# An attention and two MLP layers on one core: the MLP's step counter moved one tick forward, and the first loads issued in another order

## The chip, the cores and the metric

The kernel runs on one core of one Trainium2 chip. The metric is device time in microseconds of one execution, from launch to end. The core has five queues that run by themselves and meet at semaphores: PE (TensorE, matrix products), DVE (VectorE), ACT (ScalarE), POOL (GpSimd) and SP (SyncE, which here only issues DMAs). ACT issues a few DMAs too. Each queue works strictly in the order of the program: an instruction that waits holds up all that stands behind it.

## What is computed

Three parts follow each other: attention inside chunks of 64 tokens, a layer with squared ReLU, and a mixture of four experts with given weights.

```python
attn = softmax(q_c @ k_c.T / sqrt(64))          # per head, per chunk of 64 tokens
x = (attn @ v_c)  ->  [2304 tokens, 512]
h = max(x @ w_in, 0); y = (h * h) @ w_out       # w_in, w_out arrive as float64
p = domain_probs / sum
out = sum_e p[:, e] * (max(y @ w1[e], 0) @ w2[e])
```

Every float32 product is made of three products of float32r parts (high x high, high x low, low x high), so each operand is split into a high part and a low rest before use. The float64 weights are first turned into float32 on the chip.

## The kernel before

**Ticks.** Attention and the first MLP layer are woven together in a loop over ticks `r` (lines 895 to 950). The 2304 tokens are 18 tiles of 128. Attention of tile t runs in four stages over three ticks: `s0_stage` (transposes q and k on PE, ACT copies them out; for tile r+1 in tick r), `s1_stage` (scores on PE; DVE takes the maximum and subtracts it, L241 and L242, two of each), `exp_stage` (ACT), `norm_stage` (DVE, L253 to L256, in the next tick), `s2_stage` (transposes of the probabilities, PE and ACT, two ticks later), `s3_stage` (product with v on PE; ACT writes the high part of x at L283, DVE the low part at L284).

**Steps.** The first layer is cut into 80 steps `m`, four passes over five blocks of tokens (384, 384, 512, 512, 512) and four columns of w_in each. Step m runs in tick r = m + `LEAD`. In it `l1(m)` makes 12 matmuls into a PSUM bank (L300), ACT applies ReLU (L311), DVE squares (L312), ACT and DVE split the result (L316, L317); `l2(m-1)` makes 12 matmuls of the step before (L333). Until tick 20 `l1` always takes the one bank of tag "h" (`psh`), which the next `l1` can enter only when L311 and L312 have read it. `LEAD` is 5: tokens 0 to 383 are tiles 0 to 2, tile 2 goes through `s3_stage` in tick 4, so step 0 in tick 5 is the first that finds its block of x.

**Weights.** A unit is a 128-wide piece of w_in or w_out (512 KB as float64). `unit_load` brings it in, `unit_convert` makes it float32 (two ACT operations, L131 and L132; four on DVE, L133, L136, L141, L144; two on POOL, L145 and L146), `unit_split` splits it one tick later (ACT L153, POOL L154). `FIRST` gives the tick of conversion of the eight units of the first pass, in the order of `order`: one in each of ticks 0 to 7. The load of a unit stands two ticks ahead of its conversion. `SECOND` does the same around the end of attention (ticks 17 to 24), `UOFF` for the later passes, relative to `LEAD`. `JOBS` are ticks in which preparation of the second layer's weights starts.

**Order within a tick.** DMAs of the tick on SP; scores of tile r; normalisation of tile r-1; first half of the conversions; three quarters of `l1`; `s2`; `s0` of q; the last quarter of `l1` with ReLU and square, and a quarter of `l2`; `s0` of k; second half of the conversions; a quarter of `l2`; `s3`; exp; splits of units; the split of the step's result and the rest of `l2`. The banks for scores and transposes are taken from eight in turn while m < 0 (`tags = "ttthaaaa"`) and from three after that (`"t"`).

**Start.** The identity matrix is built on POOL, PE runs eight warming matmuls on it, and the first loads are issued from SP and ACT in turns:

```python
two = (nc.sync, nc.scalar)
run_all([load_qk(0, two)])        # q of tile 0 on SP, k on ACT
unit_load(*order[0])              # SP
run_all([load_qk(1, two)])
unit_load(*order[1])              # SP
run_all([load_v_chunk(0, c, two) for c in range(2)])
```

The later loads are all on SP. The program gives each DMA one of eight completion semaphores in turn, so an issue waits until the DMA eight places earlier has landed.

Of the kernel before, what the change touches and what calls it, by code (L numbers as in the profile page):

```python
# [10 lines left out]
F32 = mybir.dt.float32  # L11
# [7 lines left out]
P = 128  # L19
# [2 lines left out]
G = 4  # L22
LAG = 1
RING = 6
LEAD = 5
QK_BUFS = 3
ACC_EARLY = 3
FIRST = [0, 1, 2, 3, 4, 5, 6, 7]
WARM = 8
SECOND = [-3, -2, -1, 1, 0, 2, 3, 4]  # L30
RAW_BUFS = 4
# [2 lines left out]
NSUP = 3  # L34
LAG_A = 2
UOFF = [1, 3, 5, 16, 8, 17, 18, 19]
JOBS = [23, 26, 29, 32, 35, 44, 47, 50, 53, 56, 64, 67, 70, 73, 76, 79]
PLAIN = 16
SWAP = 67

# [6 lines left out]
def tile_kernel(ctx, tc, q, k, v, moe_w_in, moe_w_out, moe2_p, moe2_w1, moe2_w2, out):  # L47
    nc = tc.nc
# [156 lines left out]
    def load_v_chunk(b, c, engines):  # L205
        if b not in vt:
            new_v(b)
        for x in range(2):
            engines[x].dma_start(
                out=vt[b][x * CH:(x + 1) * CH, :, c, :],  # L210
                in_=v[b, x::2, c * CH:(c + 1) * CH, :].rearrange("j k d -> k j d"),
            )
            yield
# [599 lines left out]
    def run_all(loads):  # L813
        for y in loads:
            if hasattr(y, "__next__"):
                for _ in y:
                    pass

    with tc.manual_schedule():
        ident = const.tile([P, P], F32, name="ident")  # L820
        make_identity(nc, ident)
        warm = bank("t")
        for _ in range(WARM):
            nc.tensor.matmul(warm[:, :P], lhsT=ident, rhs=ident, start=True, stop=True)

        two = (nc.sync, nc.scalar)
        run_all([load_qk(0, two)])
        unit_load(*order[0])
        run_all([load_qk(1, two)])
        unit_load(*order[1])  # L830
        run_all([load_v_chunk(0, c, two) for c in range(2)])
        def load_dp():
            late["dp"] = late["x"].tile([P, NTILE, E], F32, name="dp")
            nc.sync.dma_start(out=late["dp"], in_=moe2_p.rearrange("(t p) e -> p t e", p=P))
# [9 lines left out]
                out=prob, in0=dp, in1=psum_.to_broadcast([P, NTILE, E]), op=ALU.mult  # L844
            )

        at(NTILE + 14, "load", load_dp)
        at(NTILE + 20, "split", probs)

        def mlp(m):  # L850
            if 0 <= m < NS:
# [43 lines left out]
        for r in range(LEAD + NS + LAG):  # L895
            m = r - LEAD
            tags = "ttthaaaa" if m < 0 else "t"
            ch = mlp(m) if m >= 0 else iter(())
            if r == NTILE + LAG_A:
                att.close()  # L900
                late["x"] = ctx.enter_context(tc.tile_pool(name="xq", bufs=1, side="right"))
# [5 lines left out]
            if r < NTILE + LAG_A:  # L907
                if r < NTILE:
                    s1_stage(r, tags)
                if 0 <= r - 1 < NTILE:  # L910
                    norm_stage(r - 1)
                conv = do(r, "convert")
                for c in conv:
                    next(c)
                run(ch, 3)
                if 0 <= r - LAG_A:
                    s2_stage(r - LAG_A, tags)
                if r + 1 < NTILE:
                    s0_stage(r + 1, tags, 0)
                run(ch, 2)  # L920
                if r + 1 < NTILE:
                    s0_stage(r + 1, tags, 1)
                for c in conv:
                    run(c)
                run(ch, 1)
                if 0 <= r - LAG_A:
                    s3_stage(r - LAG_A, tags)
                if r < NTILE:
                    exp_stage(r)
                do(r, "split")  # L930
            else:
                if r == SWAP:
                    staging.close()
                    late["raw"] = raw_pool.enter_context(tc.tile_pool(name="raw", bufs=1, reuse_waits="tile"))
                for fn, args in early.pop(r, ()):
                    fn(*args)
                if r > y0_at:
                    next(late.setdefault("y0", y_combine(0)), None)
                if m < NS:
                    run(ch, KD + 2)  # L940
                    conv = do(r, "convert")
                    for c in conv:
                        next(c)
                    run(ch, 1)
                    for c in conv:
                        run(c)
                    do(r, "split")
# [101 lines left out]
```

## Time and profile before

| | us |
|---|---|
| median of three runs | 1227.51 (1227.33 to 1228.13) |
| the profiled execution | 1227.66 |
| its span, first to last instruction | 1225.9 |
| PE busy | 1201.9 (98%) |
| DVE busy | 799.3 (65%) |
| ACT busy | 586.3 (48%) |
| POOL busy | 688.2 (56%) |

The profiled execution lies 0.15 above the median; 1.76 us of it lie outside the span. The page's shares are means over stages that differ: the first 50 us, where attention has no MLP to run beside it, look unlike the rest, so they have to be read by stretches.

### The profile page before, as it was taken

What the parts mean: (1) busy time and instruction counts of PE and PEld (TensorE: products, weight loads), DVE (VectorE), ACT (ScalarE), POOL (GpSimd) and SP (SyncE); (2) the same over time, 40 slices, a digit from 0 to 9 for tenths busy, and PEclk for the clock granted to TensorE, in tenths of its full rate; (3) what the DMA queues carried; (4) which work ended last, traced back from release to release, by engine and by line L of the source; (5) the groups of instructions that cost most, each with busy time, mean ns of one, the idle gap of its engine ahead of it and who ended that gap; (6) DMA issues with size and microseconds to landing.
All of it is one profiled execution on the core that took longest, in us unless ns stands there. A gap on an engine that the chain in (4) does not pass through costs nothing.

```text
span 1225.9 us, 20909 instructions
## 1 busy us (share of the span) xinstructions
PE 1201.9 (98%) x7912; PEld 1108.7 (90%) x7912; DVE 799.3 (65%) x1336; ACT 586.3 (48%) x1172; POOL 688.2 (56%) x650
## 2 busy tenths in 40 slices
PE   7899999999999999999999999999999999999997
PEld 5798888889888988898889889999999999999996
DVE  6966666656747566355555555676767776767676
ACT  5654555534534335533333345454445654545453
POOL 3510157717735465766776644666756766566665
PEclk7999999999999999999999999999999999999999
DMA  9955033552462645555555448666666676666653
GB/s 207 197 124 146 18 91 115 182 189 86 172 216 88 203 155 190 196 189 189 189 189 189 171 152 324 256 255 251 247 248 257 245 291 243 241 241 246 250 226 112
DMA packets 134709, 238.38 MB, mean 194 GB/s; under 512 B 64720, under 2 KB 109776, under 8 KB 128464
## 3 DMA queue, kind: packets, MB, share of 16 engines
q1 hardware_dynamic: 131984, 236.39, 55.8%
q8 instruction: 62, 1.02, 0.3%
q10 hardware_dynamic: 2624, 0.66, 0.3%
q14 instruction: 39, 0.32, 0.1%
HBM read 173.58 MB, written 63.44 MB: 193 GB/s over the span
## 4 chain that ended last, share of the span: by engine, by line
PE 89%; DVE 6%; DMA 2%; issue 1%; ACT 1%; POOL 1%; DVEq 0%; ACTq 0%; SPq 0%; POOLq 0%
PE pst L563 23%; PE psa L658 18%; PE psa L333 15%; PE psa L675 11%; PE pst L300 9%; PE psh L300 6%; PE psh L563 4%; DMA k<-in_k 2%; PE pst L276 1%; PE pst L220 1%; PE pst L235 1%; DVE uw L713 1%; PE pst L262 0%; DVE o L757 0%; DVE o L756 0%
## 5 line engine op out<-in xcount | busy, mean ns | idle before, releaser
L563 PE MATMUL pst<-ar 128*128 128x384 f32 x1728 | 344.5, 336 | 0.4 <-ACT u L596 0.4
L563 PEld LDWEIGHTS pst<-ar 128*128 128x128 f32 x1728 | 295.7, 188 | 8.0 <-ACT u L596 0.7
L333 PE MATMUL psa<-ar 128*128 128x512 f32 (+1 forms) x960 | 219.3, 372 | 1.6 <-ACT ar L316 0.8
L333 PEld LDWEIGHTS psa<-ar 128*128 128x128 f32 x960 | 173.6, 188 | 27.7 <-ACT ar L316 2.2
L589 POOL TENSOR_TENSOR ar<-s,ar 128x384 fp32r<-128x384 f32 x128 | 129.7, 1024 | 64.5 <-ACT ar L588 62.6
L675 PE MATMUL psa<-ar 128*128 128x512 f32 x576 | 149.0, 394 | 0.0
L658 PE MATMUL psa<-ar 128*128 128x256 f32 x1008 | 140.4, 283 | 1.7 <-DVE uw L707 0.7
L658 PE MATMUL psa<-w2x,ar 128*128 128x256 f32 x1008 | 135.6, 279 | 3.2 <-DVE uw L711 2.4
L658 PEld LDWEIGHTS psa<-ar 128*128 128x128 f32 x1008 | 134.4, 188 | 3.7 <-DVE uw L713 1.6
L658 PEld LDWEIGHTS psa<-w2x,ar 128*128 128x128 f32 x1008 | 130.8, 189 | 4.8 <-DVE uw L711 2.6
L145 POOL TENSOR_TENSOR raw<-raw 128x512 f32<-128x512 f32 x32 | 34.3, 1073 | 179.1 <-DVE raw L144 73.3
L689 DVE SCALAR_TENSOR_TENSOR o<-psa,prob,o 128x512 f32<-128x512 f32 x90 | 67.6, 751 | 94.2 <-PE psa L675 94.1
L300 PE MATMUL pst<-ar 128*128 128x512 f32 (+1 forms) x576 | 127.2, 369 | 0.0
L675 PEld LDWEIGHTS psa<-ar 128*128 128x128 f32 x576 | 106.6, 188 | 16.8 <-DVE ar L578 0.2
L596 ACT COPY u<-pst 128x384 f32<-128x384 f32 x144 | 69.4, 482 | 103.5 <-PE pst L563 101.9
L300 PEld LDWEIGHTS pst<-ar 128*128 128x128 f32 x576 | 105.4, 188 | 14.3
L607 ACT ACTIVATE ar<-psh 128x384 fp32r<-128x384 f32 x96 | 47.2, 492 | 140.9 <-DVE psh L603 74.1
L725 POOL TENSOR_TENSOR o<-o,x 128x256 f32<-128x256 f32 x89 | 70.4, 791 | 70.5 <-ACT x L721 68.3
L511 POOL TENSOR_TENSOR ar<-raw,ar 128x896 fp32r<-128x896 f32 x32 | 68.0, 2126 | 74.4 <-ACT ar L510 74.4
L588 ACT CAST ar<-s 128x384 fp32r<-128x384 f32 x128 | 65.5, 513 | 61.6 <-DVE s L584 59.0
L300 PE MATMUL psh<-ar 128*128 128x512 f32 (+1 forms) x384 | 88.9, 373 | 0.4 <-DVE ar L284 0.4
L713 DVE TENSOR_TENSOR uw<-psa,uw 128x512 f32<-128x512 f32 x96 | 63.4, 688 | 31.4 <-PE psa L658 20.6
(132 smaller groups left out, 1899.9 us busy)
## 6 DMA issues: line engine op xcount, KB each, us to landing
ar<-w1d SPq DMA_DIRECT2D x32, 1792.0 KB, 7.3
w2d<-jsplit SPq DMA_DIRECT2D x64, 448.0 KB, 3.5
w1d<-ar SPq DMA_DIRECT2D x16, 1792.0 KB, 8.4
ar<-w2d SPq DMA_DIRECT2D x32, 896.0 KB, 7.9
w2x<-w2d SPq DMA_DIRECT2D x32, 896.0 KB, 8.1
raw<-in_moe_w_in SPq DMA_DIRECT2D x16, 512.0 KB, 4.7
raw<-in_moe_w_out SPq DMA_DIRECT2D x16, 512.0 KB, 5.0
raw<-in_moe_w SPq DMA_DIRECT2D x16, 512.0 KB, 4.4
```

The source lines that it names most:

```text
L300: nc.tensor.matmul(ph[:, :T], lhsT=w[:, kk, :], rhs=x[tb][:, kk, :], start=(kk == 0 and n == 0), stop=(kk == KD - 1 and n == 2),)
L333: nc.tensor.matmul(o, lhsT=w, rhs=y, start=(f == 0 and n == 0), stop=(f == G - 1 and n == 2))
L511: nc.gpsimd.tensor_tensor(out=l, in0=a, in1=h.bitcast(F32), op=ALU.subtract)
L563: nc.tensor.matmul(p, lhsT=w[:, kk, :], rhs=y[:, kk, :], start=(kk == 0 and z == 0 and u in (0, 1, 3)), stop=(kk == 1 and z == 2 and u in ...
L588: nc.scalar.copy(h, st[n, nm])
L589: nc.gpsimd.tensor_tensor(out=l, in0=st[n, nm], in1=h.bitcast(F32), op=ALU.subtract)
L596: nc.scalar.copy(s, d if at == 3 else b)
L658: nc.tensor.matmul(p, lhsT=w, rhs=y, start=(k in (1, 7) and z == 0), stop=(k in (3, 4) and z == 2), skip_group_check=True,)
L675: nc.tensor.matmul(p, lhsT=w[:, ts], rhs=y[:, i, :], start=(i == 0 and z == 0), stop=(i == 1 and z == 2))
L689: nc.vector.scalar_tensor_tensor(out=o, in0=p, scalar=pe, in1=o, op0=ALU.mult, op1=ALU.add)
L713: nc.vector.tensor_tensor(out=uw, in0=pb[n, t, 0], in1=uw, op=ALU.add)
L725: nc.gpsimd.tensor_tensor(out=o1[:, :2 * P], in0=o1[:, :2 * P], in1=x, op=ALU.add)
```

## The change

`LEAD` becomes 4, and step 0 is not run in its tick 4 but whole at the head of tick 5's MLP work, ahead of step 1, which is in tick 5 now. So from step 1 on every step runs one tick sooner against attention. The conversions of units (1,1), (3,0), (2,1) and (3,1) move one tick sooner, so that tick 3 has two and tick 7 none; their loads move with them. `JOBS`, and the two small pieces of the second layer, move by one with the steps; `SECOND` and `SWAP` stay at their ticks. At the start, a tile of one column is set by POOL ahead of the identity and copied onto itself by ACT, which makes ACT load its function table there; q and k of tiles 0 and 1 are all issued on SP, and the first two chunks of v (four DMAs) all on ACT, behind that copy.

```diff
-LEAD = 5
+LEAD = 4
-FIRST = [0, 1, 2, 3, 4, 5, 6, 7]
+FIRST = [0, 1, 2, 3, 3, 4, 5, 6]
-JOBS = [23, 26, 29, 32, 35, 44, 47, 50, 53, 56, 64, 67, 70, 73, 76, 79]
+JOBS = [22, 25, 28, 31, 34, 43, 46, 49, 52, 55, 63, 66, 69, 72, 75, 78]
...
     with tc.manual_schedule():
+        dot = const.tile([P, 1], F32, name="dot")
+        nc.gpsimd.memset(dot, 1.0)
         ident = const.tile([P, P], F32, name="ident")
         make_identity(nc, ident)
...
-        two = (nc.sync, nc.scalar)
-        run_all([load_qk(0, two)])
+        one = (nc.sync, nc.sync)
+        run_all([load_qk(0, one)])
+        nc.scalar.copy(dot, dot)
+        run_all([load_v_chunk(0, c, (nc.scalar, nc.scalar)) for c in range(2)])
         unit_load(*order[0])
-        run_all([load_qk(1, two)])
+        run_all([load_qk(1, one)])
         unit_load(*order[1])
-        run_all([load_v_chunk(0, c, two) for c in range(2)])
...
-        at(NTILE + 14, "load", load_dp)
-        at(NTILE + 20, "split", probs)
+        at(NTILE + 13, "load", load_dp)
+        at(NTILE + 19, "split", probs)
...
-            ch = mlp(m) if m >= 0 else iter(())
+            ch = mlp(m) if m > 0 else iter(())
...
                 for c in conv:
                     next(c)
+                if m == 1:
+                    run(mlp(0))
                 run(ch, 3)
```

## Rows read from the trace of the kernel before

**Rows 1.** The page, part 1: busy us (share of the span) of each engine

```profile
PE 1201.9 (98%) x7912; PEld 1108.7 (90%) x7912; DVE 799.3 (65%) x1336; ACT 586.3 (48%) x1172; POOL 688.2 (56%) x650
```

**Rows 2.** Busy time by stretch: length, PE, PEld, DVE, ACT, POOL, clock, DMA, GB/s

```profile
36.00:48.00 12.00, 10.61 (x158) 9.74 (x155) 11.62 (x24) 8.60 (x17) 5.94 (x5) 0.88 0.91 198
48.00:56.00 8.00, 8.00 (x102) 7.29 (x103) 7.26 (x18) 4.77 (x10) 4.47 (x5) 1.00 0.83 180
```

**Rows 3.** The chain that ended last, 47 to 56 us: start, us, what

```profile
47.91 0.63 PE pst L220 x4
48.54 0.54 PE psh L300 x3
...
50.58 1.08 PE pst L276 x32
...
52.90 0.91 PE pst L235 x30
53.81 1.79 PE psh L300 x9
55.59 0.44 PE pst L262 x4
```

**Rows 4.** Waits of DVE, 0 to 50 us: us in total, times, longest

```profile
DVE mx L241 <- PE psh L235: 8.6, 2, 8.0
DVE mx L241 <- PE psa L235: 1.0, 1, 1.0
DVE ar L284 <- ACT ar L283: 0.5, 1, 0.5
```

**Rows 5.** Waits of PE, 0 to 50 us

```profile
PE pst L220 <- DVE e L242: 1.0, 1, 1.0
```

**Rows 6.** Timeline, 36 to 45 us: start, us, engine, instruction, [idle before]

```profile
38.23 0.68 DVE L284 TENSOR_TENSOR ar<-psh,ar 128x512 fp32r<-128x512 f32 x1
...
38.97 1.86 PE L300 MATMUL psh<-ar 128*128 128x384 f32 x9 [0.41 <-DVE ar L284]
...
40.83 1.27 POOL L154 TENSOR_TENSOR ar<-cv,ar 128x512 fp32r<-128x512 f32 x1
...
41.12 1.02 DVE L254 TENSOR_SCALAR sm<-sm 128x8 f32<-128x8 f32 x1
...
43.82 0.55 DVE L312 SCALAR_TENSOR_TENSOR r<-psh,r 128x384 f32<-128x384 f32 x1
```

**Rows 7.** Timeline, 14 to 32 us, DVE: one L254, a conversion's first and last

```profile
14.94 0.17 DVE L254 TENSOR_SCALAR sm<-sm 128x8 f32<-128x8 f32 x1
...
29.49 0.42 DVE L133 TENSOR_SCALAR cv<-cv 128x512 f32<-128x512 f32 x1
...
31.14 0.43 DVE L144 TENSOR_SCALAR raw<-cv 128x512 int32<-128x512 int32 x1
```

**Rows 8.** Timeline, 0 to 6 us: DMA issues of ACT and its first work

```profile
0.72 1.24 ACTq L186 DMA_DIRECT2D k<-in_k  x2
...
1.99 2.50 ACTq L209 DMA_DIRECT2D v<-in_v  x2
...
4.53 1.28 ACT L224 ACT_TABLE_LOAD   x1 [4.53 <-issue]
...
5.82 0.58 ACT L224 COPY qT<-pst 128x512 f32<-128x512 f32 x1
```

**Rows 9.** The chain in its first 16 us: transfers of k for tiles 1 and 2

```profile
1.26 7.14 DMA k<-in_k
...
8.85 6.20 DMA k<-in_k
```

**Rows 10.** Busy time by stretch, 36 to 40 us, for the clock (columns of Rows 2)

```profile
36.00:38.00 2.00, 2.00 (x50) 2.00 (x48) 1.90 (x5) 0.78 (x3) 0.00 (x0) 0.50 1.30 262
38.00:40.00 2.00, 1.59 (x19) 1.40 (x15) 1.97 (x5) 2.00 (x4) 1.48 (x2) 0.80 0.92 157
```

**Rows 11.** Busy time by stretch, just after attention (columns of Rows 2)

```profile
210.00:220.00 10.00, 9.16 (x48) 7.88 (x47) 8.02 (x16) 5.35 (x11) 5.43 (x5) 1.00 0.62 215
```

## What the change will do to the time

> **What bounds the kernel now.** I read the busy shares first: PE is busy 98% of the span and no other engine over 65% [rows 1]. That is a mean, and it leaves 24 us in which PE is not busy, so the next view is the busy time by stretch. From 48 to 56 us PE is busy all the time (8.00 of 8.00), while in 36 to 48 it is busy for 10.61 of 12.00 and DVE for 11.62 [rows 2]. The chain of work that ended last says the same: behind the start it runs along DVE, and at 47.91 it goes over to PE and stays there through the rest of attention [rows 3]. So the kernel has two stages. In the first, DVE does attention's maxima, normalisation and the conversion of the weights and hardly stops; in the second PE is never short of work. An edit of the order pays only by what it takes out of PE's idle time.
>
> The point that matters is where the first layer starts. Its first matmul is at 38.97, right behind the low part of x of tile 2 (L284, 38.23 to 38.91) [rows 6]. I call 38.91 T0. Both kernels execute the same PE work from there on: the same attention stages of tick 5 and later, the same 80 steps, the same second layer. Only two things can then move the end: T0 itself, and PE's idle time behind T0.
>
> **What the change can win behind T0.** Between 38.97 and 47.91 (8.94 us) PE does nine matmuls of `l1`, a transpose group s2, one s0, three matmuls, an s0, the product with v, the scores, nine matmuls, and one s2. With the back-to-back times of the chain: 1.79 + 0.44 + 0.44 + 0.54 + 0.44 + 1.08 + 0.91 + 1.79 + 0.44 = 7.87 [rows 3]. (For an s0 I use the 0.44 of s2, the same four transposes.) Idle: 8.94 - 7.87 = 1.1 us; the waits of PE name nearly all of it, 1.0 for the maxima of tile 6 [rows 5]. After 47.91 there is none. So the step that is pulled forward can fill 1.1 us, however much work it brings: 24 matmuls in tick 5 only push later ones back. **Gain 1.1.**
>
> **What it costs behind T0.** In tick 5 all of step 0 now stands ahead of step 1, and both use the one bank psh. PE does the twelve matmuls of step 0 in 12/9 x 1.79 = 2.4 us and then waits at the first matmul of step 1 until L312 has read the bank; queued behind it on PE are s2, s0, s3 and the next scores. On DVE, L312 keeps its place behind the four operations of the scores, the four of normalisation and the first half of a conversion. In the trace of before it ends at 43.82 + 0.55 = 44.37, which is 5.46 after T0 [rows 6]. So PE stands 5.46 - 0.06 (T0 to first matmul) - 2.4 = 3.0 us. In before, s2, s0 and the last three matmuls filled this time. **Loss 3.0.** Bounds: the normalisation holds an L254 of 1.02 us that sits until POOL's L154 ends (40.83 + 1.27 = 42.10), where an undisturbed one takes 0.17 [rows 6, 7]; without that meeting the loss is 2.2, with another such one 3.9. Behind the wait I see nothing that holds PE again: the second step's own L312 comes behind only its last three matmuls, while PE still has s0, half of l2, s3 and the scores to do.
>
> **What happens to T0.** DVE is the path to T0. Up to T0 five units were converted (ticks 0 to 4); now six are, as tick 3 has two. One conversion holds DVE from 29.49 to 31.57, **2.1 us** [rows 7], and its second half stands ahead of L284 on DVE. Its POOL work is added too: the second unit's L144 comes up while POOL works on the first's L145. I take 0.3 for that, between nothing and the 0.85 by which a disturbed L254 exceeds an undisturbed one [rows 6, 7]. Against it stand DVE's waits: 0.6 (8.6 less the first 8.0), 1.0 and 0.5, together 2.1 [rows 4]. These hang on the loads. The chain begins with one transfer of k after the other, with k of tile 2 issued only at 8.85, after k of tile 1 (1.26 + 7.14 = 8.40) had landed [rows 9]. In the new order q and k are not behind v and the second unit, the four v are early in ACT's queue, and the semaphore that the q of tile 2 takes is that of an earlier transfer; I expect tiles 1 to 3 to arrive about 1 us sooner. I take 1.6 of the 2.1 as won: the 1.0 and the 0.6 whole, the 0.5 not, since that one waits for PE and ACT within the tick. So T0 moves by 2.1 + 0.3 - 1.6 = **+0.8**. Bounds: all of 2.1 won and a start 0.35 sooner gives -0.35; nothing won and 0.85 of contention gives +2.95. The further 512 KB that lands before tile 5 does (one unit more) is in this range as well: DVE's tick 3 is longer by just about as much.
>
> **The table load and the first copies.** In before ACT issues two k (1.24) and two v (2.50), then loads its table (1.28, 4.53 to 5.81), and copies qT at 5.82 [rows 8]. Now it loads the table, copies the dot and issues four v: 0.72 + 1.28 + about 0.2 + 4 x 1.25 = 7.2 at the price of those two v, 5.0 at the price of a k (0.62 + a little). PE's transposes allow the copy at about 5.5. I take no shift, as both orders put the same kinds of work ahead of it; bounds -0.3 and +1.4. The memset of the dot on POOL delays the identity by at most its own 0.2 or so, an estimate from the same bound.
>
> The Trainium skill speaks against this part in "ScalarE: Activation LUTs" (What ACT_TABLE_LOAD costs): a switch costs about 1.28 us of load and 1.38 of drain, 2.66 together. The row disagrees for this first load, since the copy starts 0.01 behind its end [rows 8]. By the page ACT would be free 1.4 later and the sum would be +4.1; by the row it stays +2.7.
>
> **Edits that I cost at nothing.** `JOBS`, the probabilities and the later units move with the steps. `SECOND` stays at its ticks, so its last split (tick 25) is now three ticks ahead of its first use instead of four, and its POOL work meets the first job one tick more. The cover is ample, but PE's 0.84 of idle time in 210 to 220 is from this crowded part [rows 11]; it may vanish or double, so I add 0.8 either way to the range. Step 16 in tick 20 now follows directly on the low part of x of tile 17; between them PE has six matmuls of l2, at 0.2 each 1.2 us (more, as they are wider) against a copy of 0.58 and an L284 of 0.68 [rows 3, 6, 8]. They cover it; at worst it shows 0.1.
>
> **Sum.** +0.8 + 3.0 - 1.1 = +2.7. Against the profiled execution (span 1225.9, with 1.76 around it 1227.66) that is 1230.4; this execution lies 0.15 above the median of the runs, so I predict **1230.2**.
>
> **Rivals.**
> (1) *The loads pay in full*: the path to T0 loses all 2.1 of DVE's waits, and with the row of normalisation undisturbed the wait for psh is 2.2. -0.35 + 2.2 - 1.1 = +0.75, or +1.6 with the disturbed one: about 1228.6, no slower by the measure. It decides as soon as T0 comes at 39.4 or sooner. For it: the chain shows that loads set the first 15 us (8.85 + 6.20). Against it: DVE's waits are only 2.1 in all, and the added conversion eats them.
> (2) *ACT is held by its v issues*: the first copies come up to 1.4 later, for the four v at 1.25 each; it decides once the qT copy starts after 6.3. +2.7 + 1.4 = +4.1, 1231.6. For it: the 1.25 of the rows; against it: those two issues stood beside SP's.
> (3) *The reordering does nothing*: the same bytes come at the same rate, DVE's waits stay, T0 moves by 2.4. +2.4 + 3.0 - 1.1 = +4.3, 1231.8. The Trainium skill's "DMA: Bandwidth & Descriptors" (Issuing engines are not separate DMA queues) speaks for it: which engine issues saves only issue time.
> (4) *The clock drops in the new gap.* Between 36 and 38 the granted clock was 0.50, the lower of the two levels (1.2 of 2.4 GHz), and in the next two 0.80 on the mean, so full again after 0.8 of them [rows 10]; PE's transposes had waited for loads before it. Should the 3.0 us of idle bring it on for these 2.8 us once more, half of them is lost: +2.7 + 1.4 = +4.1, 1231.6.
> (5) *Faster by over 0.2%*, 1225.0 or less: by the working above PE's idle time behind T0 allows 1.1 and T0 0.35, together 1.5 even with no wait for psh. It needs something that this trace does not show.
>
> **How the numbers follow.** Forecast 0.38 (its own range 1229.2 to 1231.2), rival 1 0.27, rival 2 0.13, rival 3 0.10, rival 4 0.07, rival 5 0.05. A measurement of this kernel tells about 0.2%, 2.46 us, from no change: above 1229.97 is slower. Of the forecast's 0.38 I count 0.25 above that line; with rivals 2 to 4 slower is 0.55, the rest of the forecast and rival 1 give 0.40 for the same, 0.05 for faster. The range goes from rival 1's low end, +0.75, less 0.8 for the part after attention and rounded down to 1227.0, up to +2.95 + 3.9 - 1.1 = +5.75, 1233.3, rounded to 1233.5.
>
> **What would show it.** In the profile after: L284 of tile 2 ends near 39.7; the first twelve matmuls of L300 are followed by a PE wait of about 3 us that names DVE's L312; behind it PE is busy without a gap; two conversions lie in DVE's tick 3; DVE's waits for the scores fall from 1.6 to near 0. What would make it wrong: no wait of PE for L312 or T0 at 38 or earlier would mean that I misread the order in tick 5, or the loads' part; a PE that waits again in ticks 6 to 8 would add to the loss.

## The result and the profile after

The changed kernel takes 1243.9 us (median; 1243.3 to 1245.5) against 1227.8 for the kernel before; the ratio on record is 1.0126, interval 1.0114 to 1.0139. The forecast was 1230.2, +2.7 us; the result is +16, far outside the range of 1227.0 to 1233.5. The profiled execution took 1243.42, its span is 1241.6, 15.75 longer than before's.

The first part of the page after (columns of [rows 1]): PE is busy for 12.3 us more, though it executes the same 7912 matmuls. So part of the loss is not waiting; matmuls themselves took longer.

```profile
PE 1214.2 (98%) x7912; PEld 1120.5 (90%) x7912; DVE 801.1 (65%) x1336; ACT 587.6 (47%) x1173; POOL 692.4 (56%) x651
```

Busy time by stretch of the kernel after, the two stretches of [rows 2] and that of [rows 11]: behind the start PE is now short of work in both, and just after attention as well, each time with a lower granted clock (the column ahead of the last two).

```profile
36.00:48.00 12.00, 8.45 (x84) 7.24 (x84) 11.58 (x21) 5.00 (x10) 8.48 (x8) 0.72 0.72 173
48.00:56.00 8.00, 6.82 (x48) 6.45 (x50) 3.03 (x7) 2.77 (x5) 0.00 (x0) 0.79 1.09 202
...
210.00:220.00 10.00, 7.98 (x35) 7.40 (x34) 6.45 (x10) 5.47 (x12) 8.70 (x9) 0.83 0.21 79
```

The waits of PE after, 36 to 60 us (columns of [rows 4]), name the wait that was forecast, L300 for L312:

```profile
PE psh L300 <- DVE r L312: 2.6, 1, 2.6
PE pst L220 <- DVE e L242: 2.3, 1, 2.3
PE psh L300 <- DVE ar L284: 1.6, 1, 1.6
```

**Where the time went.** A total can't tell that; the start of the same piece of work in both traces can. The table takes the end of L284 of tile 2 (T0), the first matmul (L300) of steps 16, 28 and 79, and the end of the span, each minus the same in before (38.91; 165.10; 223.76; 481.94; 1225.88). Steps before the 16th are left out, since attention lies beside other steps in the two kernels there.

| kernel | ratio to before (interval) | T0 | step 16 | step 28 | step 79 | end |
|---|---|---|---|---|---|---|
| the change | 1.0126 (1.0114 to 1.0139) | +4.0 | +8.7 | +12.2 | +12.0 | +15.8 |
| lead_only | 1.0089 (1.0074 to 1.0104) | +3.5 | +8.9 | +12.4 | +12.2 | +12.3 |
| lead_nopool | 1.0073 (1.0059 to 1.0086) | +1.9 | +7.4 | +10.8 | +10.6 | +10.1 |
| lead_bank | 1.0045 (1.0030 to 1.0060) | +3.5 | +4.4 | +7.8 | +7.6 | +7.4 |
| lead_firstlate | 1.0067 (1.0052 to 1.0082) | 0.0 | +5.6 | +9.0 | +8.8 | +8.3 |
| lead_second | 1.0050 (1.0033 to 1.0066) | +3.2 | +8.8 | +8.8 | +8.6 | +8.6 |
| lead_all3 | 1.0034 (1.0021 to 1.0047) | +0.5 | +6.3 | +6.3 | +6.0 | +5.7 |
| lead_all3_s2 | 1.0021 (1.0012 to 1.0030) | -0.2 | +5.6 | +4.1 | +3.9 | +3.9 |
| lead_bank_second | 1.0022 (1.0013 to 1.0032) | +3.6 | +4.6 | +4.5 | +4.3 | +4.3 |
| dot_right | 1.0083 (1.0068 to 1.0098) | +3.5 | +8.5 | +12.0 | +11.7 | +11.4 |
| loads_only | 1.0041 (1.0025 to 1.0057) | +1.4 | +1.5 | +1.6 | +1.6 | +5.7 |
| loads_right | 1.0029 (1.0017 to 1.0040) | +3.1 | +6.1 | +6.1 | +6.1 | +6.0 |
| pad32 | 1.0029 (1.0018 to 1.0040) | -0.7 | +0.1 | +0.1 | +0.1 | +4.2 |
| pad64 | 1.0034 (1.0023 to 1.0045) | +0.3 | +0.3 | +0.3 | +0.3 | +4.5 |
| pad_w2x | 1.0005 (0.9997 to 1.0014) | +0.5 | +2.5 | +2.5 | +2.5 | +3.0 |
| pad_accp | 0.9998 (0.9989 to 1.0007) | +0.2 | +0.2 | +0.2 | +0.2 | +0.2 |
| before_second | 0.9989 (0.9980 to 0.9998) | +0.4 | +1.0 | -0.4 | -0.4 | -0.5 |

The last five kernels leave the order of the first loads as it was, and still their T0 lies between -0.7 and +0.5 and step 16 of one, pad_w2x, at +2.5. pad_w2x even turned out to be the same program as the kernel before (see its section), so +2.5 is what two executions of one program can differ by. Over 27 executions the kernel before took 1227.1 to 1231.7, median 1229.5, and the profiled one, from which all these differences are taken, is one of the short ones (1227.7). A difference of that size in one profile is no finding; the ratios, over several runs, decide there.

In the row of the change stand three separate losses: 8.7 up to step 16, 3.5 between steps 16 and 28, 3.7 behind step 79 (and 0.2 come back between 28 and 79). The forecast had only the first, at 2.7.

**Up to step 16.** The timeline of DVE after; [rows 6, 7] have the same operations of before:

```profile
32.84 0.44 DVE L144 TENSOR_SCALAR raw<-cv 128x512 int32<-128x512 int32 x1
...
33.90 1.15 DVE L144 TENSOR_SCALAR raw<-cv 128x512 int32<-128x512 int32 x1
...
38.84 1.48 DVE L256 TENSOR_TENSOR e<-e,sm 128x512 f32<-128x512 f32 x1
...
42.22 0.68 DVE L284 TENSOR_TENSOR ar<-pst,ar 128x512 fp32r<-128x512 f32 x1
...
46.39 1.48 DVE L256 TENSOR_TENSOR e<-e,sm 128x512 f32<-128x512 f32 x1
...
48.58 0.55 DVE L312 SCALAR_TENSOR_TENSOR r<-psh,r 128x384 f32<-128x384 f32 x1
```

T0 is 42.90. The second conversion is there, and both L144 of tick 3 with it; the later one takes 1.15. The normalisation's L256 takes 1.48 in tick 4 and in tick 5, where it took 0.69 in before. The timeline of PE after, L300 alone:

```profile
40.88 0.44 PE L300 MATMUL psh<-ar 128*128 128x384 f32 x1
...
42.96 3.66 PE L300 MATMUL psh<-ar 128*128 128x384 f32 x11 [1.63 <-DVE ar L284]
...
49.18 2.51 PE L300 MATMUL psh<-ar 128*128 128x384 f32 x9 [2.56 <-DVE r L312]
```

Step 1 enters psh 6.28 after T0. Then nine matmuls take 2.51 that took 1.79 in [rows 3], since the clock is at its lower level (1.2 GHz) there. Busy time by stretch, after:

```profile
43.00:47.00 4.00, 3.62 (x11) 3.11 (x11) 3.83 (x8) 0.87 (x2) 3.92 (x4) 0.57 0.55 121
50.00:53.00 3.00, 3.00 (x14) 2.90 (x14) 0.26 (x1) 0.42 (x1) 0.00 (x0) 0.51 1.36 217
...
213.00:217.00 4.00, 3.80 (x12) 3.54 (x13) 1.60 (x2) 1.94 (x4) 4.00 (x4) 0.62 0.00 0
```

The sum is 4.0 (T0) + 2.8 (idle behind T0) + 1.9 (the rest) = 8.7. Of the 1.9 some 1.7 is the clock: 3.4 us at half speed behind the wait. The 2.8: from T0 to step 1's entry 6.28, less 12 matmuls of 2.4, is 3.9; less the 1.1 of idle that before had there. The eleven matmuls of step 0 that ran at half speed between 43 and 47 lie inside the wait and cost nothing: in lead_only the same eleven ran at full speed in 2.20, the wait was 4.0 instead of 2.6, and step 1 entered psh 6.28 after T0 as well.

**Steps 16 to 28.** The first use of step 22's split result waits, and then runs at half clock. Timeline after:

```profile
201.10 0.72 DVE L133 TENSOR_SCALAR cv<-cv 128x512 f32<-128x512 f32 x1 [0.57 <-ACT cv L131]
...
204.43 0.85 DVE L144 TENSOR_SCALAR raw<-cv 128x512 int32<-128x512 int32 x1
...
206.94 0.91 DVE L133 TENSOR_SCALAR cv<-cv 128x512 f32<-128x512 f32 x1
...
211.05 0.43 DVE L144 TENSOR_SCALAR raw<-cv 128x512 int32<-128x512 int32 x1
...
211.93 0.56 DVE L312 SCALAR_TENSOR_TENSOR pst<-pst,r 128x384 f32<-128x384 f32 x1
...
213.05 4.27 PE L333 MATMUL psa<-ar 128*128 128x384 f32 x12 [1.87 <-ACT ar L316]
```

Timeline of DVE before, the conversion and L312 of the same step 22:

```profile
196.38 0.88 DVE L133 TENSOR_SCALAR cv<-cv 128x512 f32<-128x512 f32 x1
...
199.46 0.43 DVE L144 TENSOR_SCALAR raw<-cv 128x512 int32<-128x512 int32 x1
...
200.34 0.56 DVE L312 SCALAR_TENSOR_TENSOR pst<-pst,r 128x384 f32<-128x384 f32 x1
```

The conversion ahead of L312 of step 22 is the first of the third pass, which moves with the steps and stands there in both kernels. The one from 201.10 to 205.28 is the last of `SECOND`: it stands ahead of L312 of step 21 now, and stood ahead of that of step 20 in before, where step 21 had none. So two conversions follow each other directly, and the later one meets POOL's work for the earlier: it takes 4.5 us (206.94 to 211.48) where it took 3.5 (196.38 to 199.89), and L312 of step 22 starts 7.3 after the first matmul of its step instead of 4.4.

**Behind step 79.** In the second layer one form of matmul takes longer, each of 1008 alike. Groups by line, before (form, busy, mean ns):

```profile
L658 PE MATMUL psa<-w2x,ar 128*128 128x256 f32 x1008 | 135.6, 279 | 3.2 <-DVE uw L711 2.4 <-DVE uw L713 0.7
```

and after:

```profile
L658 PE MATMUL psa<-w2x,ar 128*128 128x256 f32 x1008 | 139.8, 284 | 2.4 <-DVE uw L711 2.3
```

### The profile page after: what moved, and what is told of

The parts are those of the page before. It is cut to its first block, busy times and chain, and to the rows that moved or that the text cites. A ratio compares the mean times of both kernels' runs of the same rounds, so it can differ in the third digit from the quotient of the medians.

```text
span 1241.6 us, 20899 instructions
## 1 busy us (share of the span) xinstructions
PE 1214.2 (98%) x7912; PEld 1120.5 (90%) x7912; DVE 801.1 (65%) x1336; ACT 587.6 (47%) x1173; POOL 692.4 (56%) x651
## 3 DMA queue, kind: packets, MB, share of 16 engines
q8 instruction: 62, 1.02, 0.3%
## 4 chain that ended last, share of the span: by engine, by line
PE 89%; DVE 5%; DMA 2%; POOL 1%; issue 1%; SPq 1%; ACT 1%; DVEq 0%; POOLq 0%; ACTq 0%
PE pst L563 23%; PE psa L658 18%; PE psa L333 15%; PE psa L675 11%; PE pst L300 8%; PE psh L300 6%; PE psh L563 4%; PE pst L276 1%; DMA k<-in_k 1%; PE pst L220 1%; PE pst L235 1%; SPq L209 1%; PE pst L262 1%; DVE o L756 0%; POOL raw L145 0%
## 5 line engine op out<-in xcount | busy, mean ns | idle before, releaser
L333 PE MATMUL psa<-ar 128*128 128x512 f32 (+1 forms) x960 | 221.4, 374 | 3.4 <-ACT ar L316 3.0
L333 PEld LDWEIGHTS psa<-ar 128*128 128x128 f32 x960 | 174.7, 189 | 29.3 <-ACT ar L316 3.9
L589 POOL TENSOR_TENSOR ar<-s,ar 128x384 fp32r<-128x384 f32 x128 | 132.4, 1046 | 59.6 <-ACT ar L588 57.5
L658 PE MATMUL psa<-w2x,ar 128*128 128x256 f32 x1008 | 139.8, 284 | 2.4 <-DVE uw L711 2.3
L145 POOL TENSOR_TENSOR raw<-raw 128x512 f32<-128x512 f32 x32 | 34.6, 1082 | 188.9 <-DVE raw L144 93.3
L658 PEld LDWEIGHTS psa<-w2x,ar 128*128 128x128 f32 x1008 | 134.9, 190 | 3.3 <-DVE uw L711 2.5
L300 PE MATMUL pst<-ar 128*128 128x512 f32 (+1 forms) x576 | 127.0, 369 | 0.0
L300 PEld LDWEIGHTS pst<-ar 128*128 128x128 f32 x576 | 105.3, 188 | 14.2
L300 PE MATMUL psh<-ar 128*128 128x512 f32 (+1 forms) x384 | 92.0, 383 | 4.2 <-DVE r L312 2.6
```

Of the source, the lines that this page charges most:

```text
L300: nc.tensor.matmul(ph[:, :T], lhsT=w[:, kk, :], rhs=x[tb][:, kk, :], start=(kk == 0 and n == 0), stop=(kk == KD - 1 and n == 2),)
L333: nc.tensor.matmul(o, lhsT=w, rhs=y, start=(f == 0 and n == 0), stop=(f == G - 1 and n == 2))
L589: nc.gpsimd.tensor_tensor(out=l, in0=st[n, nm], in1=h.bitcast(F32), op=ALU.subtract)
L658: nc.tensor.matmul(p, lhsT=w, rhs=y, start=(k in (1, 7) and z == 0), stop=(k in (3, 4) and z == 2), skip_group_check=True,)
```

## The experiments

### The halves of the change

`lead_only`: the change without its new loads and without the dot.

```diff
-        dot = const.tile([P, 1], F32, name="dot")
-        nc.gpsimd.memset(dot, 1.0)
...
-        one = (nc.sync, nc.sync)
+        two = (nc.sync, nc.scalar)
```

> The changed kernel with the first loads in the old order and without the dot: only LEAD, FIRST, JOBS and step 0 in step 1's tick. Theory (placement): T0 stays late by 3 to 4 us for the second conversion in tick 3, the wait for psh stays, the crowded stretch after attention stays, and the second layer is as in the kernel before: 1239 us. Rival (phase): the second layer still loses 3.7 us, 1243 us. Rival (loads): the lateness of T0 was mostly the loads', T0 within 1.5 us of 38.91 and 1235 us.

Measured: 1239.98, 1.0089. All of the loss up to step 79 is in this half, and nothing behind it: its w2x form takes 279 ns. The theory's 1239 held.

`loads_only`: the kernel before with the new loads and the dot.

```diff
+        dot = const.tile([P, 1], F32, name="dot")
+        nc.gpsimd.memset(dot, 1.0)
...
-        two = (nc.sync, nc.scalar)
+        one = (nc.sync, nc.sync)
```

> The kernel before with the new order of the first loads alone (the dot, its table load, q and k on SP, v on ACT); LEAD, FIRST and step 0 as before. Theory (placement): the one-column tile moves every later SBUF address by 32 bytes, and the second layer loses 3.7 us by it, while the loads themselves cost 0.3 to 0.6 us at T0 (the low part of x of tile 2, before 38.91): 1232 us. Rival (phase): the 3.7 us of the second layer come from the steps' new place against the jobs and DMAs, so they are absent here: 1228.2 us.

Measured: 1234.19, 1.0041. At step 79 it is 1.6 behind, and 4.1 more come in the second layer, as in the change. The theory of the place held; its price for the loads, 0.3 to 0.6 at T0, was too low: T0 is at +1.4. The loads that were to win 1.6 won nothing. SP's queue after (the change) shows why:

```profile
4.16 0.54 SPq L186 DMA_DIRECT2D k<-in_k  x1
```

k of tile 1 stands ninth now, and its issue waits until q of tile 0 has landed, at 4.15. It lands at 10.64, where before had it at 8.40 [rows 9]. DVE's wait for the scores of tile 1 grew from 1.0 [rows 4] to 2.5 in this kernel:

```profile
DVE mx L241 <- PE psa L235: 2.5, 1, 2.5
```

### Whose 3.7 us the second layer lost

`pad32` and `pad64`: the kernel before with a dot of one column (32 bytes) or 16 columns (64), set behind the identity and used by nobody, the loads as before. They tell the tile's place from its use, and one alignment from another.

```diff
+        dot = const.tile([P, 1], F32, name="dot")
         ident = const.tile([P, P], F32, name="ident")
         make_identity(nc, ident)
+        nc.gpsimd.memset(dot, 1.0)
```

> The kernel before with a one-column tile ahead of all others in SBUF and a memset of it on POOL behind the identity; nothing reads it. It moves the tiles behind it by 32 bytes, from a multiple of 64 to one of 32. Theory (placement): the matmuls of the second layer that read w2x grow from 279 to 284 ns on the mean, 1231.5 us, nothing else changes. Rival (phase): 1227.8 us.

> As pad32 with 16 columns, so that all addresses move by 64 bytes and stay multiples of 64. Theory (placement, by 32 against 64): 1227.8 us, w2x matmuls at 279 ns. Rival (any new address, or the memset itself, costs it): the same time as pad32.

Measured: 1232.28 and 1232.56, 1.0029 and 1.0034. Both are level to step 79 and lose 4.1 and 4.2 behind it. So it is the place and not the loads; that 64 bytes would bring the alignment back fell. In the built programs `ar` begins at byte 1664 of each partition before, at 1696 in pad32 and in the change, and at 1728 in pad64; `w2x` begins at 157504 in all of them. Groups by line of pad32:

```profile
L658 PE MATMUL psa<-w2x,ar 128*128 128x256 f32 x1008 | 139.8, 284 | 3.0 <-DVE uw L711 2.3 <-DVE uw L713 0.7
```

`dot_right`: the whole change with the dot taken from attention's own pool, so that no other tile moves.

```diff
-        dot = const.tile([P, 1], F32, name="dot")
+        dot = qkp.tile([P, 1], F32, tag="dot", name="dot", bufs=1)
```

> The changed kernel, the one-column tile taken from the pool of attention's tiles at the other end of SBUF, so that no other address moves. Theory (placement): the matmuls of w2x are back at 279 ns and the drift of 3.7 us in the second layer is gone, 1240 us. Rival (the table load and the new order of loads shift the second layer's phase): 1243.9 us as the changed kernel.

Measured: 1239.32, 1.0083: the loss behind step 79 is gone, with the memset and the copy still there. Against lead_only (1.0089) the new loads then make no difference that can be told.

`pad_w2x` and `pad_accp`: 32 unused bytes ahead of w2x, or behind ar, where they move the first accumulators, rp and the staging tiles.

```diff
+                        late["b"].tile([P, 8], F32, name="wpad")
                         late["w2"] = late["b"].tile([P, 2, NW], F32R, name="w2x")
```

```diff
+    accp.tile([P, 8], F32, name="apad")
     rp = ctx.enter_context(tc.tile_pool(name="rp", bufs=1))
```

> The kernel before with a tile of 32 bytes that nothing uses laid ahead of w2x, so that w2x moves by 32 bytes and ar, with all the other tiles of the program's start, stays. With ar moved by 32 or 64 bytes against w2x the matmuls of L658 that read w2x took 281 ns for 276, and the time rose by 4. If the distance of the two operands of a matmul counts, or w2x has one good place, the same matmuls now take 281 and the time is 1232.5 to 1233. Rival: only the place of ar counts (or of what lies with it); then they stay at 276 and the time at 1228.6.

> The kernel before with a tile of 32 bytes that nothing uses laid behind ar and the accumulators: rp and the weights' staging tiles move by 32 bytes, ar and w2x stay. If ar's place against w2x is what slowed the second layer, nothing changes: 276 ns for the matmuls with w2x, 1228.6. Rival: it was the place of a tile behind ar (r, the staging tiles): 281 ns and 1232.5.

Measured: 1230.25 and 1229.63, 1.0005 and 0.9998, no change; the w2x form takes 278 and 279 ns. pad_accp rules out the tiles behind ar. pad_w2x decides nothing: in the built program w2x still begins at byte 157504, because its pool is laid against the upper end of SBUF and grows downwards, so that the unused tile lies below w2x and moves nothing. It is the kernel before, run once more.

So the place of ar counts, by itself or by its distance from w2x. The same line of the kernel has a second form, with both operands in ar, which move together. Groups by line, before:

```profile
L658 PE MATMUL psa<-ar 128*128 128x256 f32 x1008 | 140.4, 283 | 1.7 <-DVE uw L707 0.7 <-DVE uw L711 0.4 <-DVE uw L713 0.3
```

and pad32:

```profile
L658 PE MATMUL psa<-ar 128*128 128x256 f32 x1008 | 140.4, 283 | 1.2 <-DVE uw L711 0.4 <-DVE uw L713 0.3 <-DVE uw L707 0.2
```

It stays at 283 ns, though its weights (the operand that stays in TensorE) moved with ar too. This speaks for the distance between the two operands and against the place of the weights alone, but no run moves w2x, so it stays open, and so does why the other place costs 5 ns per matmul.

### Where T0 went

`lead_nopool`: lead_only with POOL's L145 and L146 left out for the two units converted in tick 3. What is left out is only the low part of these weights, not all of them as the text below suggests.

```diff
-        nc.gpsimd.tensor_tensor(out=lf, in0=hi.bitcast(F32), in1=lf, op=ALU.mult)
-        nc.gpsimd.tensor_tensor(out=af, in0=af, in1=lf, op=ALU.add)
+        if (n, which) not in ((2, 0), (1, 1)):
+            nc.gpsimd.tensor_tensor(out=lf, in0=hi.bitcast(F32), in1=lf, op=ALU.mult)
+            nc.gpsimd.tensor_tensor(out=af, in0=af, in1=lf, op=ALU.add)
```

> The pull forward without the new loads, and POOL's part of the two conversions of tick 3 left out (L145 and L146 of units (2,0) and (1,1): their weights are wrong, and the work of these four POOL instructions, 1.0 to 1.4 us each, isn't done). With it T0 was 42.38. Theory: DVE's L144 of 1.16 and L256 of 1.47 (0.43 and 0.69 elsewhere), and L254 of 0.74 to 0.99, were long because POOL worked at the same time. Without the four, L144 takes 0.43 (-0.73) and at least one of the two in tick 4 takes its usual time (-0.6 to -0.8): T0 at 40.9 to 41.1, with 2.1 of the second conversion left, and the time some 1.3 to 1.5 below the 1239.98 of the kernel with POOL's part. Rival: these operations are long for a reason of their own (what they read, or what DVE waits for inside them): T0 stays at 42.3 and only POOL is idler, 1239.9.

Measured: T0 at 40.77 for 42.38, 1238.44 for 1239.98. Timeline of DVE in lead_only:

```profile
33.35 1.16 DVE L144 TENSOR_SCALAR raw<-cv 128x512 int32<-128x512 int32 x1
...
37.31 0.74 DVE L254 TENSOR_SCALAR sm<-sm 128x8 f32<-128x8 f32 x1
...
38.32 1.47 DVE L256 TENSOR_TENSOR e<-e,sm 128x512 f32<-128x512 f32 x1
```

and the same three in lead_nopool, whose lines from 145 on have numbers one higher:

```profile
32.68 0.43 DVE L144 TENSOR_SCALAR raw<-cv 128x512 int32<-128x512 int32 x1
...
36.88 0.17 DVE L255 TENSOR_SCALAR sm<-sm 128x8 f32<-128x8 f32 x1
...
37.33 0.69 DVE L257 TENSOR_TENSOR e<-e,sm 128x512 f32<-128x512 f32 x1
```

The three operations are 0.73, 0.57 and 0.78 shorter, as expected of POOL's presence and not of themselves. T0 comes only 1.6 sooner, since the low part of x (L284) of tick 3 then waits 0.76 for ACT. The Trainium skill says in "SBUF — State Buffer" (Who interferes with whom) that a DVE operation in a two-port mode and a GpSimd operation block each other for a whole instruction, and that a DVE operation with two inputs in SBUF contends with a GpSimd operation that reads SBUF. These rows agree; in which mode DVE worked no row shows.

`lead_firstlate`: lead_only with the second conversion back in tick 4, so that T0 has only before's five conversions ahead of it.

```diff
-FIRST = [0, 1, 2, 3, 3, 4, 5, 6]
+FIRST = [0, 1, 2, 3, 4, 5, 5, 6]
```

> lead_only with FIRST = [0, 1, 2, 3, 4, 5, 5, 6]: the two conversions of one tick stand in tick 5, behind T0 (the low part of x of tile 2), not in tick 3. Theory (the second conversion is what makes T0 late): T0 comes back from 42.4 to about 39.5, L312 of step 0 is later against T0 by 0.9, and 2 us come back, 1238 us. Rival (T0 is late for the loads and the clock): T0 stays over 41.5 and the time at 1240 us or above it.

Measured: 1237.96, 1.0067, as the theory had it. T0 is back at 38.93, and 3.3 of the 8.9 at step 16 are won, not more: tick 5 has two conversions now, and PE waits twice for POOL's splits of weights (L154) behind them. Waits of PE, 40 to 70 us:

```profile
PE psh L300 <- DVE r L312: 3.2, 1, 3.2
PE psh L300 <- POOL ar L154: 1.8, 1, 1.8
PE psa L333 <- POOL ar L154: 0.8, 1, 0.8
```

### The wait for psh

`lead_bank`: lead_only with step 0 in a bank of tag t.

```diff
-            ph = bank("h" if "x" not in late else "httt")
+            ph = bank("t" if i == 0 else "h" if "x" not in late else "httt")
```

> lead_only (1240.0, all of the change but the first loads) with step 0 of the first layer in a bank of tag t in place of psh, so that step 1 needs no L312 before it starts. Theory (the wait for psh is paid in full): lead_only's wait of 4.0 us is gone, nothing else takes its place, 1236 us. Rival (DVE is the bound there): PE then waits in tick 5 or 6 for DVE's maxima or for L316 and L317, and under 1.5 us come back, 1238.5 to 1240 us.

Measured: 1234.86, 1.0045. Step 1 starts at 44.68, right behind step 0 (42.43, 2.42 long), and 4.5 at step 16 come back with T0 unchanged, 1.1 us more than the theory had. The granted clock stays at 1.00 from 48 to 56 us:

```profile
48.00:56.00 8.00, 6.71 (x89) 5.78 (x90) 4.84 (x11) 5.66 (x11) 3.69 (x3) 1.00 1.01 226
```

Here the wait and the fall of the clock behind it are gone together; what is left behind T0 is a first use of step 0's split, 1.3 of L333 for L316. It doesn't follow that the wait for psh is what brings the fall. Of the six kernels in which PE waits for psh, five have the lower clock within that wait or behind it (the change, lead_only, lead_nopool, lead_second, dot_right), and lead_firstlate, which waits 3.2, has not. Busy time by stretch of lead_firstlate, behind its wait:

```profile
45.00:56.00 11.00, 11.00 (x122) 10.18 (x121) 7.70 (x15) 6.47 (x14) 5.55 (x5) 1.00 0.97 195
```

And it falls without any wait for psh: in pad_w2x, the same program as the kernel before, behind a wait of 2.4 for the low part of x of tile 2. Before, where that wait was 0.41:

```profile
40.00:43.00 3.00, 3.00 (x34) 2.76 (x34) 2.86 (x6) 1.50 (x4) 2.10 (x2) 1.00 0.35 78
```

and pad_w2x:

```profile
40.00:43.00 3.00, 3.00 (x12) 2.91 (x12) 2.86 (x7) 0.00 (x0) 2.54 (x3) 0.50 0.37 81
```

So a stretch of 3.4 us at half speed, 1.7 us, can come or not come in one and the same program. Each of those named here stands behind a wait of PE, but not every wait has one behind it.

### The stretch after attention

`lead_second`: lead_only with the conversions around the end of attention one tick sooner, so that step 21 has none again.

```diff
-SECOND = [-3, -2, -1, 1, 0, 2, 3, 4]
+SECOND = [-4, -3, -2, 0, -1, 1, 2, 3]
```

> lead_only with SECOND one tick sooner, so that the second pass's conversions keep their place against the steps and the jobs. Theory (the crowded stretch after attention comes from SECOND staying while steps and jobs move): steps 23 to 27, which lose 3.4 us more against the kernel before in lead_only, lose nothing, 1236.5 us. Rival (the clock falls there by itself or the jobs alone crowd POOL): the loss of 3.4 stays, 1240 us.

Measured: 1235.54, 1.0050; step 28 stands where step 16 stood (+8.8). The 3.5 are gone whole, as the theory had it. Busy time by stretch in lead_second, against 7.98 at clock 0.83 after:

```profile
210.00:220.00 10.00, 9.76 (x55) 9.08 (x53) 6.74 (x10) 4.10 (x9) 8.70 (x10) 1.00 0.45 152
```

`before_second`: the same edit in the kernel before.

> The kernel before with nothing changed but the conversions after attention, one tick sooner (the list SECOND). If PE's idle time in 200 to 220 us comes from splits that arrive just too late, as the loss of 3.5 us in the changed kernel and its absence with the same list one tick sooner say, then 0.5 to 1.0 us goes: about 1227.8, step 28 at -0.5 to -1.0. Rival: what is idle there is set by the meeting of POOL's and ACT's work itself, which only moves with the list: no change, 1228.6, or a new wait among attention's last ticks and 1229.5.

Measured: 1228.12 against 1229.5, 0.9989 (0.9980 to 0.9998). Between steps 24 and 28 it gains 1.4. It is the one kernel here whose interval lies below 1; at 0.1% it can barely be told from the kernel before.

```profile
210.00:220.00 10.00, 9.64 (x52) 8.51 (x51) 8.05 (x16) 5.35 (x11) 5.85 (x5) 1.00 0.68 231
```

### All repairs together

`lead_all3` joins the three edits above (bank, `FIRST`, `SECOND`) on lead_only; `lead_all3_s2` has `SECOND` another tick sooner; `lead_bank_second` leaves `FIRST` as in the change.

```diff
-SECOND = [-4, -3, -2, 0, -1, 1, 2, 3]
+SECOND = [-5, -4, -3, -1, -2, 0, 1, 2]
```

> The pull forward without the new loads, with all three repairs at once: step 0 of the first layer in a bank of tag t instead of psh, the second conversion of tick 3 put back into tick 4 (and the next two both in tick 5), and the conversions after attention one tick sooner as well. My theory is that the three losses have three places and add up: T0 at 38.9 as in the kernel before; no wait of PE on psh; step 16 at about +0.95 (what the kernel with only the other bank lost behind its T0: 4.41 - 3.46), the stretch from step 16 to step 28 flat; no slower second layer. Together +0.5 to +1.0, 1229 to 1229.6. Rival: with the T0 of before the second conversion of tick 5 still stands on DVE and POOL ahead of step 0's square and split, so that taking away the wait for the bank only moves it to the 12 matmuls of l2 that need step 0's split (L333 waiting for L316, L317 or POOL): step 16 at +2 to +4, 1230.5 to 1232.5.

> As the kernel with the three repairs, but with the conversions after attention two ticks sooner than in the kernel before, so one tick sooner against the first layer's steps than there. If PE's idle time between 200 and 220 us of the kernel before (0.84 in one stretch of 10) hangs on how close these splits stand to their first use, it goes too, and this kernel is 0.5 to 0.9 below the one with the three repairs: about 1228.5, even with the kernel before. Rival: two ticks sooner the conversions fall among attention's last ticks, where DVE and POOL are fuller, and hold PE there: step 16 later by 1 or more, 1230.5 and above.

> The pull forward without the new loads, with step 0 in a bank of tag t and the conversions after attention one tick sooner. The bank alone had step 16 at +4.41 and step 28 at +7.84; the sooner conversions alone kept what was at step 16 level to step 28. Theory: both hold together, step 16 and step 28 at +4.4, end at +3.7: 1231.5 to 1232. That is below the kernel with all three repairs (1233.39), since putting the second conversion back into tick 4 only moves it to where step 0 waits. Rival: the sooner conversions meet work that the other bank has let come earlier, step 28 at +6 or more: 1233.5 or above.

Measured: 1233.39, 1232.02 and 1232.07. My sum for lead_all3 fell: step 16 is at +6.3, worse than its rival allowed, though T0 is within 0.5. Waits of PE in lead_all3, 40 to 70 us:

```profile
PE psh L300 <- POOL ar L154: 1.8, 1, 1.8
PE psa L333 <- ACT ar L316: 1.5, 1, 1.5
PE psa L333 <- POOL ar L154: 0.9, 1, 0.9
```

These are 4.2 us, where before waits 1.0 in this window. The conversion moved out of tick 3 is paid by POOL, whose splits then come late for their first use, as in lead_firstlate, and by the clock behind the longest of the three. Busy time by stretch in lead_all3:

```profile
64.00:67.00 3.00, 3.00 (x14) 2.90 (x13) 1.24 (x4) 0.69 (x2) 0.35 (x1) 0.50 0.02 5
```

lead_all3_s2 has the same two waits for L154. It is 1.4 below lead_all3, more than the 0.5 to 0.9 expected, and in the traces the stretch from step 16 to step 28 gives as much; the 1228.5 fell with the sum of lead_all3. lead_bank_second did as expected. None of the three reaches the kernel before.

### The loads without the dot's place

`loads_right`: loads_only with the dot in attention's pool, its memset behind the identity.

> The kernel before with only the new order of the first loads and ACT's table loaded ahead, the one-column tile placed among attention's own tiles, so that no tile of the second layer moves. Theory: the loads by themselves cost what the earlier run of the loads alone showed up to 750 us, T0 at 40.3 and step 16 at +1.5, as k of tile 1 is now issued on SP only after q of tile 0 has landed; and with no tile moved nothing is lost in the second layer: 1230.1. Rival: the whole change with the tile placed this way had step 16 at 8.49, against 8.92 without the new loads, so the loads are neutral or a little better and T0 stays at 39: 1228.6.

Measured: 1233.13, 1.0029 (1.0017 to 1.0040); both values fell. The w2x form is back at 279 ns, but step 16 is at +6.1. Timeline of ACT:

```profile
1.37 0.78 ACTq L209 DMA_DIRECT2D v<-in_v  x1
...
4.13 5.42 ACTq L209 DMA_DIRECT2D v<-in_v  x3
9.60 0.58 ACT L224 COPY qT<-pst 128x512 f32<-128x512 f32 x1 [7.39 <-DMA v<-in_v]
```

Here the issue that waits for q of tile 0 is not that of k on SP but the second v on ACT; the last of the four v is issued at 8.95, when q of tile 1 has landed (8.93), and ACT comes to the qT copy 3.8 later than in [rows 8]. This ends as the second rival of the prediction, ACT held by its v issues, at nearly three times its price, but through waits for semaphores and not through the length of the issues. T0 is at +3.1 behind it. The other 3.0 of the 6.1 come with the clock, without any wait for psh. Busy time by stretch:

```profile
42.00:48.00 6.00, 5.98 (x22) 5.79 (x23) 4.73 (x10) 1.20 (x3) 3.07 (x3) 0.50 0.94 212
```

Why the small difference of place in POOL's queue moved the wait to another issue I have not settled, so this run doesn't price the order of the loads by itself.

## Why the prediction was wrong

The forecast of +2.7 misses 13 us in six places: T0 +3.2, the wait for psh +0.9, the rest up to step 16, mostly the clock, +1.9, `SECOND` +3.5, the dot's place +3.7, and 0.2 that come back. Behind a part of it stands a premise of the prediction: both kernels execute the same PE work, so that only T0 and PE's idle time can move the end. PE was busy for 12.3 us more; the same matmuls took longer, by the clock and by the place of a tile.

**T0, +0.8 forecast, +4.0 measured.** The step that failed first is the credit for the loads. I took 1.6 of DVE's waits as won, on the assumption that the semaphore for tile 2's q would be that of an earlier transfer; I followed the eight semaphores to tile 2 and not to k of tile 1, the ninth issue, which waits for the first transfer. Tick 3 begins 0.5 later than before, so the term is +0.5 for -1.6. The third rival had it that the reordering does nothing, with the Trainium skill's "DMA: Bandwidth & Descriptors" (Issuing engines are not separate DMA queues); dot_right against lead_only, 1.0083 and 1.0089, agrees. The second conversion itself was sized right: from the first conversion's start to L284 tick 3 takes 4.45 for 1.99 in before, +2.46, against 2.1 + 0.3. What I left out is that DVE's normalisation meets POOL in other places than before: in ticks 3 and 4 its four operations take 2.58 and 3.11 (27.94 to 30.52 and 37.14 to 40.25), 0.55 and 0.53 more than the 2.03 and 2.58 of before. In tick 4 it is POOL's work of the second conversion, and the split that stands behind it, that reaches so far; lead_nopool shows it. In tick 3 that work has not begun (the first L145 starts at 33.41), and L254 meets the split of an earlier unit. 0.5 + 2.46 + 0.55 + 0.53 = 4.0.

**The wait for psh, +1.9 forecast with the 1.1 that it fills, +2.8 measured.** The mechanism was right, place and name. The size is that of the bound that I gave, "with another such one 3.9": 3.9 - 1.1. L254 meets POOL as in before (1.00 for 1.02), and L256 now meets it too (1.48 for 0.69).

**The clock, a rival of 0.07, +1.9.** It came behind the wait, 3.4 us at the lower level for the 2.8 that I took, about 1.7. Two facts lay in [rows 10]: a lower clock after PE had waited for loads, and its price. I kept it out of the sum, and five of the six kernels with a wait for psh have it. That this wait is its cause is not shown (see lead_bank): lead_firstlate waits and keeps its clock, pad_w2x and loads_right lose it without this wait. What decides it stays open.

**`SECOND` at nothing, +3.5.** I named it, wrote "the cover is ample" and bounded it at 0.8 from the 0.84 of idle in [rows 11]. I looked at the first use of its splits and at the first job, and not at its neighbour: the shift by one tick put the last conversion of `SECOND` directly ahead of the first one of the third pass. PE waits 1.87 for step 22's split, and 3.4 us at the lower clock follow, 1.7 more. As I read it now, the 0.84 was itself the sign that the cover was used up (before_second wins 1.4 there). lead_second took all of it back.

**The dot, +3.7.** I priced its instructions (right: 0.10 and 0.19) and not that it moves other tiles in memory. Nothing in the trace of before shows this; the range could not have held it.

**The first table load.** After it ends at 2.00, and the copy of the dot starts at 2.01. The Trainium skill's "ScalarE: Activation LUTs" (What ACT_TABLE_LOAD costs) states 1.38 us of drain beside the load for a switch; no run here shows one at this place. The load was moved off the path, and nothing came of it, since the qT copy waits for q's transposes (5.96 after, 5.82 before).

**What the whole change was worth.** With nothing gained from the loads, and 1.1 of idle time the most that the earlier step could fill, there was nothing to set against these. Even lead_bank_second, with psh and the crowded stretch mended and the first loads and tile places of before, stays slower (1232.07 against 1229.54): DVE is the bound before T0, and the change gives it a conversion more there. Put behind T0, as in lead_all3, that conversion holds PE there.

## What to carry to other kernels

Before work is pulled forward into a stretch, look which engine is full there: one whose busy time is 11.6 of 12 us pays for each moved operation in whole, and its neighbour that works at the same time is paid too. A short idle time of the engine that bounds a crowded stretch says that the cover is gone, not that little is lost; look at what a shifted operation will stand next to, also in work that does not shift with it. And a new tile, however small, should not move the tiles behind it: give it a place where nothing lies above it, compare the duration of one unchanged matmul form before and after, and look up the addresses in the built program before you say what a padding moved. Last, take a second profile of the unchanged kernel: what differs between the two is no effect of a change.

## What the runs showed of the hardware

- With ar 32 or 64 bytes further on, 1008 matmuls with their weights in ar and the other operand in w2x took 284 or 285 ns instead of 279, 4 us in the whole, with the same shapes and types; 1008 of the same shape with both operands in ar stayed at 283.
- DVE operations of 0.17, 0.43 and 0.69 us took 0.74 to 1.48 while POOL ran instructions of 1.0 to 1.4 beside them; with these left out on POOL they took their usual time.
- After a wait of PE of 2.56 us the granted clock was 0.51 from 50 to 53 us, while PE was busy all the time (3.00 of 3.00); after one of 3.2 in lead_firstlate it was 1.00 from 45 to 56. In one and the same program (before and pad_w2x) it was 1.00 or 0.50 from 40 to 43 us, behind a wait of 0.41 or 2.4.
